# Linear attention and a gated long convolution: forward DFT ahead of the second projection, on quarters of the sequence, with all steps in a new order

## The chip, the cores and the metric

The kernel runs on one core of one Trainium2 chip. The metric is the device time of one execution in microseconds. Before the change the median of three runs is 329.52 us (328.03 to 329.56).

## What is computed

Inputs are q, k, v of shape (8 batches, 8 heads, 576 tokens, 64), a feature matrix `w_phi` (64 x 128), and for the second half `w_proj` (512 x 1536), a filter (576 x 512) and `w_out` (512 x 512). All are float32; the kernel works in bf16 with float32 sums. Per batch:

```python
def phi(x):                                   # x is q or k, per head
    p = x @ w_phi
    p = p - max(abs(p), axis=-1)
    return concat([exp(p), exp(-p)])
kv, z = phi(k).T @ v, sum(phi(k), axis=tokens)
x = (phi(q) @ kv) / (phi(q) @ z + 1e-6)        # 8 heads side by side: 576 x 512
x1, x2, x3 = split(x @ w_proj, 3)              # 576 x 512 each
conv = irfft(rfft(x2, axis=tokens) * rfft(filter, axis=tokens))
out = (x1 * conv * x3) @ w_out
```

## The kernel before, in words

The whole program is one list of words, `PLAN`. Each word is a step with its arguments: `X2,3,1@2` calls method `X2` for batch 3, chunk 1, with its result in PSUM bank 2; `#1` names one of the ring slots of a staging buffer. `run` walks through the list, and so the order of the list is the order of the instructions on every engine and on the DMA queues of SyncE (SP) and GpSimd (POOL). No scheduler changes it; the engines wait for each other through semaphores only where data or buffers require it. The words of several batches are interleaved: while batch b is in its attention part, batch b-1 is in its convolution part, and the last products of batch b-2 or b-1 are written out.

Tokens are taken as 64 groups (t) of 9 (j), so that a load of one batch is a plain block; a chunk of 128 tokens is two j of 64 t, and the ninth j makes a tail of 64 tokens. Steps of a batch, in the order of the data:

- `load`/`loadh` (L518, L524): DMA from POOL's queue, with a cast to bf16. `trh` (L534): DMA transposes on SP's queue, which turn q and k into `qT` and `kT`. For the first two batches the transposes are made on TensorE (PE) instead (`tp`, L553) and copied out of PSUM (`tpe`, L734 on ACT or L736 on DVE).
- `Pk`, `Qn` (L606, L613), `Pkt`, `Qnt` (L620): projections on `w_phi` in eight matmuls per two heads. `maxk`, `maxq` (L673): absolute maxima on VectorE (DVE). `mhi`, `mlo`, `trm` split the maxima of q in two bf16 halves and transpose them to `mT`; `Pq` (L634, L640) computes the transposed projection of q and subtracts the maxima with a selector matrix. `ex` (L657), `exkt`, `exqt`: exponentials on ScalarE (ACT). `em` (L708) writes exp of the maxima of k as a scale, and `vs` (L714) multiplies v by it on POOL.
- `KV` (L729), `KVe` (L736): sums over the tokens and their eviction. `NE`, `NEt` (L750, L759): numerator and denominator; `rc`, `xn`, `rct`, `xnt` (L764 to L781): division on DVE, giving `xn` (four chunks of 128 tokens) and `xnt` (tail). `trx`, `trxt` (L788, L793): DMA transposes on SP to `xT` and `xTt`, with the features on the partitions.
- `fold`, `foldt` (L808, L814) on POOL: the sums and differences of the two halves of the sequence, from `xT`, into `eo`. Even frequencies need only the sums, odd ones only the differences.
- `X2` (L820): second projection, 5 chunks x 4 matmuls of 512 columns, from `eo`. `X2e` (L734 on ACT, L736 on DVE): five evictions to `x2n`. `F` (L446): forward DFT from `x2n` with the tables `fwd`, `fwd5` as weights, 17 matmuls of 512 columns. `m12` (L831), `m1` (L837): products with the filter's spectrum on DVE, read straight from PSUM, into `Y` and `Y4`. `m3` (L842): the sum of the two halves of the complex product, mostly on POOL.
- `X1`, `X3` (L848), `X1t`, `X3t` (L855): first and third projection from `xT`, 16 matmuls of 512 columns each and tails; `X1e` evicts, `tm`, `tmt` (L885, L889) multiply on DVE.
- `I` (L895): inverse DFT, 24 matmuls of 288 columns; `Ie` (L898) evicts the even half on ACT, `Ip`, `Im` (L903) form sum and difference with the odd half in PSUM on DVE, into `cv`. `ym` (L914): product with x1*x3 on POOL into `yT`. `yt` puts the tails of two batches side by side. `O` (L926), `Oe` (L734), `st` (L942): last projection, eviction and stores on SP's queue.

Before the first batch, the tables are made: index rows on POOL, angles on ACT and DVE, sines on ACT (L380 to L384), masked copies on POOL (`gen_five`, L392, L394), the inverse tables as copies (`gen_inv`, L409 to L413), the forward tables as PE transposes (`tg`). The filter is loaded in 18 pieces on SP's queue, folded on POOL (`filt_fold`, L429, L431) and transformed by `H` (the same L446). `w_proj` is loaded in three parts, between other loads.

Of the kernel before, what the change touches and what calls it, by code (L numbers as in the profile page):

```python
# [16 lines left out]
SEQ = 576  # L17
# [4 lines left out]
        'rt': 2, 'xnt': 2, 'yT': 2, 'es': 2, 'cv': 2}  # L22
# [17 lines left out]
H_ev,DVE,3@7 Pqt,0@0 em,p,0,1 ex,q,m,0,1@2 Pq,0,0@4 KV,0,0@6 exqt,m,0@0 vs,p,0,1 ex,q,p,0,1@2  # L40
KVe,DVE,0,0@6 exqt,p,0@0 ex,q,m,0,0@4 vs,m,0,1 tp,q,1,1@2 Pq,0,2@0 ex,q,p,0,0@4 tpe,ACT,q,1,1@2
KV,0,1@6 ex,q,m,0,2@0 w_load,proj,1 ex,q,p,0,2@0 Pq,0,3@4 KVe,DVE,0,1@6 tp,q,1,0@3 NE,0,1@0
tpe,ACT,q,1,0@3 NE,0,0@6 rc,0,1@0 ex,q,m,0,3@4 xn,0,1@0 tp,q,1,3@2 H,1@3 rc,0,0@6 trx,0,1
ex,q,p,0,3@4 xn,0,0@6 NEt,0@0 NE,0,2@6 rct,0@0 H_ev,ACT,1@3 xnt,0,0@0 trx,0,0 NE,0,3@4 xnt,0,1@0
rc,0,2@6 H,2@0 xn,0,2@6 tpe,ACT,q,1,3@2 tp,q,1,2@1 rc,0,3@4 trx,0,2 tp,k,1,3@3 xn,0,3@4 H,4@2
tpe,ACT,k,1,3@3 tpe,DVE,q,1,2@1 H_ev,ACT,2@0 trx,0,3 Qnt,1@6 late Qn,1,0@4 maxqt,1@6 w_load,proj,2
Qn,1,2@0 maxq,1,0@4 tp,k,1,2@3 trxt,0 load,v,1 Pk,1,1@6 tpe,ACT,k,1,2@3 maxq,1,2@0 ex,k,m,1,1@6
Qn,1,1@4 ex,k,p,1,1@6 maxq,1,1@4 fold,POOL,0,1 Qn,1,3@0 X1,0,1@3 maxq,1,3@0 Pk,1,3@4 X1e,ACT,0,1@3
H_ev,ACT,4@2 fold,POOL,0,0 maxk,1,1@6 Pk,1,0@0 mhi,1 X2,0,3@3 ex,k,p,1,0@0 maxk,1,3@4 X2,0,2@2
ex,k,m,1,0@0 foldt,POOL,0,0 X2,0,0@6 foldt,POOL,0,1 X2e,ACT,0,2@2 maxk,1,0@0 load,k,3 ex,k,m,1,3@4  # L50
X2,0,4@7 mlo,POOL,1 X2e,DVE,0,3@3 load,q,2 trm,1 ex,k,p,1,3@4 X2,0,1@2 X2e,DVE,0,0@6 X2e,ACT,0,4@7
Pkt,1@0 trh,k,2,1 Pk,1,2@4 X2e,ACT,0,1@2 maxkt,1@0 X1,0,0@3 H_fix em,p,1,0 exkt,p,1@0 F,0,2@2
maxk,1,2@4 vs,p,1,0 X1e,ACT,0,0@3 F,0,0@6 em,m,1,0 exkt,m,1@0 m12,0,2@2 F,0,1@7 em,m,1,1
ex,k,m,1,2@4 F,0,4@3 vs,m,1,0 m12,0,0@6 ex,k,p,1,2@4 Pq,1,1@0 em,p,1,1 m12,0,1@7 Pqt,1@4
ex,q,m,1,1@0 F,0,3@2 vs,p,1,1 X3,0,1@6 trh,k,3,0 exqt,m,1@4 m12,0,3@2 ex,q,p,1,1@0 X3,0,0@7 tm,0,1@6
exqt,p,1@4 Pq,1,0@0 vs,m,1,1 m1,0,4@3 KV,1,0@4 ex,q,m,1,0@0 tm,0,0@7 ex,q,p,1,0@0 Pq,1,2@2
KVe,DVE,1,0@4 KV,1,1@6 m3,POOL,0,0 ex,q,m,1,2@2 Pq,1,3@4 ex,q,p,1,2@2 KVe,DVE,1,1@6 NE,1,1@0
trh,q,2,1 m3,POOL,0,1 NE,1,0@6 ex,q,m,1,3@4 rc,1,1@0 xn,1,1@0 NEt,1@2 trh,q,2,0 ex,q,p,1,3@4
rc,1,0@6 X1t,0@0 xn,1,0@6 X1te,ACT,0@0 rct,1@2 NE,1,2@6 xnt,1,0@2 trx,1,1 xnt,1,1@2 I,0,1,0@1
rc,1,2@6 NE,1,3@4 xn,1,2@6 I,0,0,0@0 trx,1,0 rc,1,3@4 X3t,0@2 xn,1,3@4 Ie,0,0@0#0 I,0,0,1@3  # L60
Ie,0,1@1#1 tmt,0@2 I,0,1,1@0 trx,1,2 Ip,0,0@3#0 I,0,2,0@1 Im,0,0@3#0 Qnt,2@6 Qn,2,0@4 Ip,0,1@0#1
Ie,0,2@1#0 Qn,2,2@2 Im,0,1@0#1 trx,1,3 X1,0,2@1 maxqt,2@6 ym,POOL,0,1 maxq,2,0@4 I,0,3,0@0
X1e,ACT,0,2@1 X1,0,3@6 trxt,1 w_load,out Ie,0,3@0#1 maxq,2,2@2 Pk,2,1@0 X1e,ACT,0,3@6 load,v,2
Qn,2,1@4 ex,k,m,2,1@0 Qn,2,3@6 maxq,2,1@4 fold,POOL,1,1 X3,0,2@2 ex,k,p,2,1@0 X1,1,1@3 maxq,2,3@6
I,0,3,1@4 X1e,ACT,1,1@3 fold,POOL,1,0 maxk,2,1@0 X3,0,3@5 mhi,2 Pk,2,3@6 Im,0,3@4#1 Pk,2,0@0
Ip,0,3@4#1 X2,1,3@3 ex,k,p,2,0@0 tm,0,2@2 foldt,POOL,1,0 foldt,POOL,1,1 X2,1,2@4 tm,0,3@5
ex,k,m,2,0@0 load,k,4 maxk,2,3@6 X2,1,0@2 X2e,ACT,1,3@3 mlo,POOL,2 ym,POOL,0,0 trm,2 X2e,ACT,1,2@4
X2,1,4@5 maxk,2,0@0 ex,k,m,2,3@6 ym,POOL,0,3 trh,k,3,1 I,0,2,1@3 X2e,DVE,1,0@2 ex,k,p,2,3@6 X2,1,1@4
load,q,3 X2e,ACT,1,4@5 Pkt,2@0 Pk,2,2@6 maxkt,2@0 X2e,ACT,1,1@4 X1,1,0@2 maxk,2,2@6 em,p,2,0
exkt,p,2@0 F,1,2@5 vs,p,2,0 X1e,ACT,1,0@2 F,1,0@4 Im,0,2@3#0 em,m,2,0 exkt,m,2@0 Ip,0,2@3#0 F,1,1@2  # L70
em,m,2,1 m12,1,2@5 ex,k,m,2,2@6 F,1,4@3 vs,m,2,0 ex,k,p,2,2@6 m12,1,0@4 Pq,2,1@0 em,p,2,1 Pqt,2@6
m12,1,1@2 ex,q,m,2,1@0 F,1,3@5 trh,k,4,0 vs,p,2,1 X3,1,1@4 exqt,m,2@6 m12,1,3@5 ex,q,p,2,1@0
X3,1,0@2 tm,1,1@4 exqt,p,2@6 Pq,2,0@0 vs,m,2,1 m1,1,4@3 KV,2,0@6 ex,q,m,2,0@0 tm,1,0@2 ex,q,p,2,0@0
Pq,2,2@4 KVe,DVE,2,0@6 KV,2,1@2 ym,POOL,0,2 ex,q,m,2,2@4 Pq,2,3@6 m3,POOL,1,0 ex,q,p,2,2@4
KVe,DVE,2,1@2 NE,2,1@0 trh,q,3,1 NE,2,0@2 ex,q,m,2,3@6 rc,2,1@0 xn,2,1@0 O,0,0@4 trh,q,3,0
ex,q,p,2,3@6 rc,2,0@2 m3,POOL,1,1 xn,2,0@2 NEt,2@0 X1t,1@5 Oe,ACT,0,0@4#0 rct,2@0 xnt,2,0@0 NE,2,2@2
trx,2,1 X1te,ACT,1@5 xnt,2,1@0 I,1,1,0@4 rc,2,2@2 NE,2,3@6 xn,2,2@2 trx,2,0 I,1,0,0@5 rc,2,3@6
X3t,1@0 xn,2,3@6 Ie,1,0@5#1 I,1,0,1@1 Ie,1,1@4#0 tmt,1@0 I,1,1,1@5 trx,2,2 Ip,1,0@1#1 I,1,2,0@4
Im,1,0@1#1 Qnt,3@2 Ip,1,1@5#0 Qn,3,0@6 Ie,1,2@4#1 Qn,3,2@0 trx,2,3 maxqt,3@2 O,0,1@4 maxq,3,0@6
X1,1,2@2 st,0,0 Im,1,1@5#0 I,1,3,0@3 maxq,3,2@0 X1e,ACT,1,2@2 ym,POOL,1,1 X1,1,3@5 trxt,2 Ie,1,3@3#0  # L80
Oe,ACT,0,1@4#1 Pk,3,1@6 X1e,ACT,1,3@5 load,v,3 Qn,3,1@2 st,0,1 Qn,3,3@0 ex,k,m,3,1@6 maxq,3,1@2
X3,1,2@4 fold,POOL,2,1 ex,k,p,3,1@6 X1,2,1@5 maxq,3,3@0 I,1,3,1@2 X1e,ACT,2,1@5 X3,1,3@3 maxk,3,1@6
fold,POOL,2,0 mhi,3 O,0,3@5 Im,1,3@2#0 Ip,1,3@2#0 Pk,3,3@0 tm,1,2@4 Oe,ACT,0,3@5#2 Pk,3,0@6
foldt,POOL,2,0 X2,2,3@2 ex,k,p,3,0@6 tm,1,3@3 foldt,POOL,2,1 load,k,5 maxk,3,3@0 X2,2,2@3
ex,k,m,3,0@6 mlo,POOL,3 ym,POOL,1,0 trm,3 X2,2,0@5 X2e,ACT,2,2@3 maxk,3,0@6 ex,k,m,3,3@0 X2,2,4@4
ym,POOL,1,3 st,0,3 X2e,DVE,2,3@2 ex,k,p,3,3@0 I,1,2,1@3 X2e,DVE,2,0@5 X2,2,1@6 load,q,4
X2e,ACT,2,4@4 O,0,2@7 X2e,ACT,2,1@6 Pkt,3@0 Oe,ACT,0,2@7#0 Pk,3,2@4 maxkt,3@0 X1,2,0@2 st,0,2
# [101 lines left out]
class Kernel:  # L189
# [258 lines left out]
    def H(self, t):  # L448
        self.dft(t, self.fe, 1)
# [550 lines left out]
```

## Time and profile before

| | |
|---|---|
| median of three runs | 329.52 us |
| the profiled execution | 332.42 us |
| its span, first to last instruction | 330.6 us |
| mean granted TensorE clock | 0.965 |
| DMA bytes moved, mean rate | 39.57 MB, 120 GB/s |

The profile comes from one execution and gives the span in several ways. *Busy time* of an engine is the time in which it had an instruction at work; PEld is the weight load of PE, which overlaps with its matmuls. A *group* line has the code line, the engine, the operation, `output<-input` with the shapes, the count, then busy time and the mean duration in ns of one instruction, then the idle time of the engine just before such instructions with what ended it. Matmuls overlap in the pipeline, so that the mean duration of one is longer than the distance from one to the next. The *chain of work* is followed back from the last instruction to whatever released each step; read forward it is a list of pieces with start, length and cause. DMA share is the mean busy share of the 16 DMA engines.

### The profile page before, as it was taken

What the parts mean: (1) busy time and instruction counts of PE and PEld (TensorE: products, weight loads), DVE (VectorE), ACT (ScalarE), POOL (GpSimd) and SP (SyncE); (2) the same over time, 40 slices, a digit from 0 to 9 for tenths busy, and PEclk for the clock granted to TensorE, in tenths of its full rate; (3) what the DMA queues carried; (4) which work ended last, traced back from release to release, by engine and by line L of the source; (5) the groups of instructions that cost most, each with busy time, mean ns of one, the idle gap of its engine ahead of it and who ended that gap; (6) DMA issues with size and microseconds to landing.
All of it is one profiled execution on the core that took longest, in us unless ns stands there. A gap on an engine that the chain in (4) does not pass through costs nothing.

```text
span 330.6 us, 9406 instructions
## 1 busy us (share of the span) xinstructions
PE 283.4 (86%) x3893; PEld 171.6 (52%) x3928; DVE 248.2 (75%) x398; ACT 226.1 (68%) x364; POOL 223.7 (68%) x186
## 2 busy tenths in 40 slices
PE   0463777898789999999997999999999989999982
PEld 0451474357434864476445754675467535844640
DVE  4487439786879698867984897988798979855750
ACT  4788766886479758984887369955896679633332
POOL 7699933794389948992979078937695749673420
PEclk9995779999999999999999899999999999999998
DMA  6778956895969887987994797996667841252146
GB/s 131 163 108 130 147 79 112 121 188 84 118 87 180 88 130 117 209 129 108 157 197 69 121 159 127 160 122 105 140 126 105 137 79 31 50 123 65 32 95 159
DMA packets 70890, 39.57 MB, mean 120 GB/s; under 512 B 51200, under 2 KB 65664, under 8 KB 70848
## 3 DMA queue, kind: packets, MB, share of 16 engines
q1 hardware_dynamic: 56032, 22.72, 38.1%
q0 software_dynamic: 14816, 16.25, 34.1%
q8 instruction: 30, 0.49, 0.6%
q14 instruction: 12, 0.10, 0.1%
HBM read 33.75 MB, written 9.44 MB: 131 GB/s over the span
## 4 chain that ended last, share of the span: by engine, by line
PE 57%; POOL 15%; DMA 11%; DVE 6%; issue 5%; ACT 4%; SPq 0%; POOLq 0%; ACTq 0%; DVEq 0%
PE ps L848 13%; PE ps L820 8%; PE ps L446 8%; PE ps L926 7%; PE ps L729 5%; PE ps L895 4%; PE ps L750 4%; DMA qT<-qn 3%; DMA xT<-xn 3%; POOL vp L714 3%; POOL vm L714 3%; DMA xTt<-xnt 2%; PE ps L634 2%; PE ps L640 2%; DMA mT<-mh 2%
## 5 line engine op out<-in xcount | busy, mean ns | idle before, releaser
L914 POOL TENSOR_TENSOR yT<-cv,x1s 128x576 bf16<-128x576 f32 x30 | 37.9, 1277 | 51.4 <-DVE cv L903 29.5
L848 PE MATMUL ps<-xT,wproj 128*128 128x512 bf16 x244 | 61.8, 380 | 2.1 <-DMA xT<-xn 1.3
L673 DVE TENSOR_REDUCE mk<-ps 128x8 f32<-128x1024 f32 (+1 forms) x40 | 43.6, 1110 | 12.4 <-PE ps L620 11.1
L673 DVE TENSOR_REDUCE mq<-ps 128x8 f32<-128x1024 f32 (+1 forms) x40 | 42.6, 1110 | 6.8 <-PE ps L613 3.5
L714 POOL TENSOR_TENSOR vp<-vn,vp 128x1152 bf16<-128x1152 bf16 x16 | 34.3, 2145 | 8.7 <-ACT vp L708 8.6
L820 PE MATMUL ps<-wproj,eo 128*128 128x512 bf16 x157 | 37.7, 380 | 2.5 <-POOL eo L814 1.5
L831 DVE TENSOR_TENSOR Y<-ps,AB 128x1024 bf16<-128x1024 f32 x32 | 36.9, 1212 | 2.9 <-PE ps L446 2.9
L657 ACT ACTIVATE Eqm<-ps 128x1024 bf16<-128x1024 f32 x32 | 33.1, 1033 | 8.0 <-PE ps L640 7.3
L808 POOL TENSOR_TENSOR eo<-xT 128x1024 bf16<-128x1024 bf16 x16 | 33.8, 2133 | 7.0 <-DMA xT<-xn 6.9
L734 ACT COPY o<-ps 128x512 f32<-128x512 f32 x36 | 21.0, 593 | 25.4 <-PE ps L926 21.7
L926 PE MATMUL ps<-wout,yT 128*128 128x512 bf16 x129 | 35.9, 385 | 2.2 <-DVE yT L914 0.9
L848 PEld LDWEIGHTS <-wproj 128*128 128x128 bf16 x256 | 23.8, 98 | 25.6
L842 POOL TENSOR_TENSOR Y<-Y 128x1024 bf16<-128x1024 bf16 x15 | 32.0, 2152 | 4.6 <-DVE Y L831 4.6
L714 POOL TENSOR_TENSOR vm<-vn,vm 128x1152 bf16<-128x1152 bf16 x16 | 34.3, 2144 | 0.0
L657 ACT ACTIVATE Ekp<-ps 128x1024 bf16<-128x1024 f32 x32 | 33.0, 1033 | 1.4 <-PE ps L606 1.3
L657 ACT ACTIVATE Ekm<-ps 128x1024 bf16<-128x1024 f32 x32 | 33.0, 1032 | 0.5 <-DVE mk L673 0.5
L657 ACT ACTIVATE Eqp<-ps 128x1024 bf16<-128x1024 f32 x32 | 33.3, 1039 | 0.0
L734 ACT CAST x1s<-ps 128x512 bf16<-128x512 f32 (+1 forms) x37 | 19.9, 538 | 18.9 <-PE ps L848 8.2
L446 PE MATMUL ps<-x2n,fwd 128*128 128x512 bf16 x134 | 31.8, 379 | 0.1
L895 PE MATMUL ps<-inv,Y 128*128 128x288 bf16 x192 | 31.1, 286 | 0.0
L898 ACT COPY es<-ps 128x288 f32<-128x288 f32 x32 | 12.0, 401 | 24.2 <-PE ps L895 13.1
L903 DVE TENSOR_TENSOR cv<-es,ps 128x288 f32<-128x288 f32 x64 | 25.6, 446 | 2.0 <-PE ps L895 1.9
(150 smaller groups left out, 593.8 us busy)
## 6 DMA issues: line engine op xcount, KB each, us to landing
out_dram<-o SPq DMA_DIRECT2D x72, 128.0 KB, 2.5
vn<-in_v_dram POOLq DMA_DIRECT2D x8, 576.0 KB, 7.8
kn<-in_k_dram POOLq DMA_DIRECT2D x7, 576.0 KB, 6.2
qn<-in_q_dram POOLq DMA_DIRECT2D x7, 576.0 KB, 8.4
wproj<-in_moe_w_proj_dram POOLq DMA_DIRECT2D x3, 512.0 KB, 6.9
fl<-in_moe_filter_fft_dram SPq DMA_DIRECT2D x18, 64.0 KB, 4.6
kn<-in_k_dram POOLq DMA_DIRECT2D x2, 288.0 KB, 6.5
qn<-in_q_dram POOLq DMA_DIRECT2D x2, 288.0 KB, 6.4
```

The lines of the kernel that those rows point to most:

```text
L446: self.mm(self.pb(0), l, r, start=(i == 0), stop=(i == len(ks) - 1))
L657: self.nc.scalar.activation(e, self.db(), AF.Exp, bias=0.0, scale=1.0 if g == "p" else -1.0)
L673: self.nc.vector.tensor_reduce(out=out, in_=src, axis=AX.X, op=ALU.max, apply_absolute_value=True)
L714: self.nc.gpsimd.tensor_tensor(out=t[:, :, :, 0:64], in0=self.at("vn", b)[:, 2 * X:2 * X + 2], in1=t[:, :, :, 64:65].to_broadcast([128, 2, ...
L734: self.nc.scalar.copy(dst, src)
L808: self.pick(eng).tensor_tensor(out=o, in0=x[:, :, :, 0, :], in1=x[:, :, :, 1, :], op=op)
L820: self.mm(self.pb(0), eo[:, kt, 128 * c:128 * c + 128], w[:, kt, 512:1024], start=(kt == 0), stop=(kt == 3))
L831: self.nc.vector.tensor_tensor(out=self.at("Y", b)[:, i, h, :], in0=self.pb(0).rearrange("p (i x) -> p i x", i=1).to_broadcast([128, 2, 512]),
L848: self.mm(self.pb(0), w[:, kt, f0 + 128 * m:f0 + 128 * m + 128], x[:, kt, :], start=(kt == 0), stop=(kt == 3))
L895: self.mm(self.pb(0, 0, 288), y, inv[:, i, :], start=(i == 0), stop=(i == 2))
L914: e.tensor_tensor(out=self.at("yT", b)[:, m, 0:SEQ], in0=self.at("cv", 4 * b + m).rearrange("p j h t -> p (j h t)"), in1=self.at("x1s", b) ...
L926: self.mm(self.pb(0), y[:, kt, 128 * j:128 * j + 128], w[:, kt, :], start=(kt == 0), stop=(kt == 3))
```

## The change

1. *The order of the two linear steps of x2 is exchanged.* A DFT over the tokens and a projection over the features commute. After the change `F` transforms `xn` itself, with the tokens on the partitions, and `X2` projects the spectrum `xf`. `F` uses the folded rows as weights and the tables as the moving operand; its result has the features on the partitions and goes through one more eviction, `Fe`, eight per batch of 288 columns; `X2` then gives 128 frequencies x 512 features in PSUM, where `m12` and `m1` read it as they read `F`'s result before. `xl` gathers the last 16 frequencies of each of the four groups into a weight for the fifth chunk of `X2`, twice side by side. `X2e` is gone.
2. *Two folds by quarters.* The token order inside a batch's chunks changes, so that a chunk's rows belong to one quarter of the sequence. `fold` forms sums (`ef`) and differences (`od`) of the halves directly from `xn`, in four instructions of 512 elements per partition; `fold2` forms sums and differences (`ee`) of the quarters from `ef`, in four of 256. An odd group of `F` is 3 matmuls of 288 columns, an even one is 2 of 144 and 1 of 288, the last of each being the unfolded tail `xnt`. The transposes of `xn` stay, for `X1` and `X3`.
3. *Layouts that follow.* `Eq`, `x1s`, `cv`, `yT`, the filter's rows and the stores have the new token order; `yt` runs for every batch into a buffer `yTt` of its own; the stores are 64 rows each as before, in pieces of 16.
4. *Tables and start.* The sines are written straight into `inv`; forward tables are PE transposes of `inv` and of small edge tables (`R`); masked copies move from POOL to DVE; the filter comes in 9 pieces. Two activations on an idle tile (`sintab`, `exptab`) are placed so that the function tables are loaded at that point, and 23 `warm` matmuls on zeros are put between the first steps.
5. *A new order of all words of `PLAN`,* which also chooses the engine anew for each movable step. Over the whole kernel, on DVE there are now 4 folds, 5 second folds, 7 `Fe`, 5 `Oe`, 3 `m3`, 1 `ym`; on POOL 28 folds, 27 second folds, 13 `m3`, 31 `ym`; on ACT 57 `Fe`, 31 `Oe`, 16 copies for `xl`. Loads of the first two batches' q and k and of the first v are in halves and earlier.

The core of the diff (the new `PLAN` is shown by its first lines and one stretch of batches 2 and 3):

```diff
+filt_load,SP,1 gen_selidx gen_rows ident gen_cols,0 zeros loadh,k,0,1 gen_cols,1 warm,2@0 sintab
+filt_load,SP,0 loadh,k,0,0 warm,4@1 loadh,q,0,1 gen_turns,0 gen_sel w_load,phi warm,4@0 gen_turns,1
+gen_angles,0 loadh,q,0,0 warm,3@1 loadh,k,1,0 warm,2@0 gen_pads gen_angles,1 gen_sin,1 loadh,q,1,0
+gen_sin,0 loadh,k,1,1 gen_ends,1 gen_sin,2 gen_selx tp,k,0,1@2 w_phi gen_ends,0 tp,k,0,0@3 warm,3@4
...
+xn,2,3@2 trh,k,4,1 I,1,1,1@4 Ie,1,1@7#0 Qn,3,0@0 fold2,POOL,2,1,0 tmt,1@5 Pk,3,0@2 Ip,1,1@4#1
+Pk,3,1@6 ex,k,p,3,0@2 fold2,POOL,2,0,0 X1,1,3@5 Im,1,1@4#1 trx,2,2 maxq,3,0@0 ym,POOL,1,1
+ex,k,m,3,0@2 O,0,0@4 trx,2,3 maxk,3,1@6 X1e,ACT,1,3@5 fold,POOL,2,0,1 I,1,0,1@1
...
-    def fold(self, eng, b, odd):
-        op = ALU.subtract if odd else ALU.add
-        x = self.at("xT", b).rearrange("p k (j h t) -> p k j h t", j=8, h=2)
-        o = self.at("eo", b)[:, :, 256 * odd:256 * odd + 256].rearrange(
-            "p k (j t) -> p k j t", j=8)
-        self.pick(eng).tensor_tensor(out=o, in0=x[:, :, :, 0, :], in1=x[:, :, :, 1, :], op=op)
...
-    def X2(self, b, c):
-        eo, w = self.at("eo", b), self.at("wproj")
+    def fold(self, eng, b, odd, p):
+        x, v = self.at("xn", b), slice(2 * p, 2 * p + 2)
+        self.pick(eng).tensor_tensor(
+            out=self.at("od" if odd else "ef", b)[:, v].rearrange("p v c x -> p v (c x)"),
+            in0=x[:, v, 0:2, :].rearrange("p v c x -> p v (c x)"),
+            in1=x[:, v, 2:4, :].rearrange("p v c x -> p v (c x)"),
+            op=ALU.subtract if odd else ALU.add)
+
+    def fold2(self, eng, b, odd, p):
+        x, v = self.at("ef", b), slice(2 * p, 2 * p + 2)
+        self.pick(eng).tensor_tensor(out=self.at("ee", b)[:, v, odd, :], in0=x[:, v, 0, :],
+                                     in1=x[:, v, 1, :], op=ALU.subtract if odd else ALU.add)
...
+    def X2(self, b, t):
+        xf, w = self.at("xf", b), self.at("wproj")
         for kt in range(4):
-            self.mm(self.pb(0), eo[:, kt, 128 * c:128 * c + 128], w[:, kt, 512:1024],
-                    start=(kt == 0), stop=(kt == 3))
-
-    def X2e(self, eng, b, c):
-        self.copy(eng, self.at("x2n", b)[:, c, :], self.pb(0))
-
-    def F(self, b, t):
-        self.dft(t, self.at("x2n", b), 0)
+            l = xf[:, kt, t, 0:128] if t < 4 else self.at("xl", b)[:, kt, :]
+            self.mm(self.pb(0), l, w[:, kt, 512:1024], start=(kt == 0), stop=(kt == 3))
+
+    def F(self, b, v, odd):
+        t = self.at("xnt", b)[:, 2 * (v // 2):2 * (v // 2) + 2, :].rearrange("p u d -> p (u d)")
+        acc = self.pb(0, 0, 288)
+        if odd:
+            o = self.at("od", b)[:, v]
+            for k in range(2):
+                self.mm(acc, o[:, k, :], self.tab(2 * k, 1), start=(k == 0), stop=False)
+        else:
+            e = self.at("ee", b)[:, v]
+            for k in range(2):
+                part = lambda x: x.rearrange("p (s f) -> p s f", s=2)[:, :, 72 * k:72 * k + 72]
+                self.mm(part(acc), e[:, k, :], part(self.tab(0, 0)), start=(k == 0), stop=False)
+        self.mm(acc, t, self.tab(1 + 2 * (v % 2), odd), start=False, stop=True)
+
+    def Fe(self, eng, b, v, odd):
+        self.copy(eng, self.at("xf", b)[:, v, 2 * odd:2 * odd + 2, :].rearrange(
+            "p g x -> p (g x)"), self.pb(0, 0, 288))
...
+    def sintab(self):
+        z = self.at("idle")[0:1, 0:1]
+        self.nc.scalar.activation(self.at("junk"), z, AF.Sin, bias=0.0, scale=1.0)
```

## The prediction

> **What bounds the kernel now.** I read the page's busy shares first, then the busy time by stage, then the chain of work, then the groups, then each engine's timeline of the first 60 us. Shares alone:
>
> ```profile
> PE 283.4 (86%) x3893; PEld 171.6 (52%) x3928; DVE 248.2 (75%) x398; ACT 226.1 (68%) x364; POOL 223.7 (68%) x186
> PE 57%; POOL 15%; DMA 11%; DVE 6%; issue 5%; ACT 4%; SPq 0%; POOLq 0%; ACTq 0%; DVEq 0%
> ```
>
> PE leads both the shares and the chain, but 86% is a mean over unlike stages. By stage (length, then busy us of PE, PEld, DVE, ACT, POOL, granted clock, DMA share, GB/s):
>
> ```profile
> 0.00:60.00 60.00, 33.29 (x512) 23.73 (x517) 37.34 (x72) 43.20 (x66) 43.82 (x59) 0.86 0.75 127
> 60.00:100.00 40.00, 34.16 (x485) 19.53 (x487) 30.84 (x46) 27.99 (x44) 26.66 (x23) 1.00 0.79 116
> 100.00:320.00 220.00, 211.93 (x2882) 126.65 (x2907) 179.74 (x281) 152.02 (x251) 153.24 (x106) 0.99 0.71 117
> 320.00:330.60 10.60, 4.02 (x17) 1.67 (x18) 0.28 (x2) 2.93 (x5) 0.00 (x0) 0.87 0.69 161
> ```
>
> Two kernels in one. In the first 60 us PE is idle for 26.7 us and POOL and ACT are busiest. From 100 to 320 PE is busy 211.9 of 220 us: there a microsecond of PE work is nearly a microsecond of time. From the start of one batch's forward DFT to the next:
>
> ```profile
> 100.00:134.20 34.20, 33.25 (x475) 20.01 (x479) 29.18 (x45) 25.89 (x44) 26.44 (x21) 1.00 0.92 133
> 134.20:168.50 34.30, 33.10 (x476) 19.92 (x479) 29.05 (x46) 25.59 (x42) 25.09 (x19) 1.00 0.96 153
> ```
>
> PE 33.1, DVE 29.1, ACT 25.7, POOL 25.8 of 34.3 us. DVE is next, 4 us behind.
>
> **Steady state, PE.** The durations of matmuls overlap (the groups' means are latencies), so I price by start-to-start, from the chain in order of time (start, length, what):
>
> ```profile
> 78.50 0.47 PE ps L759 x8
> ...
> 302.59 3.68 PE ps L446 x17
> ...
> 310.57 1.10 PE ps L895 x9
> ```
>
> One whole forward DFT of a batch is the second line: 17 matmuls of 512 columns in 3.68 us, 0.216 each. A 288-column matmul is 1.10/9 = 0.122. Of 130 columns: 0.47/8 = 0.059. No 144-column one is in the trace; it lies between 0.059 and 0.122, and by the line between them it is 0.065. The new forward DFT has per batch 4 chunks x (odd: 3 of 288; even: 2 of 144 and 1 of 288): 16 x 0.122 + 8 x 0.065 = 2.47 us. Gain 3.68 - 2.47 = 1.21 us a batch, **9.7 us** in eight. By the bounds of the 144-column price it is 8.1 to 10.1. Nothing else on PE changes in number: X2 keeps 20 x 512 columns, O its 144, the inverse its 192; Pq, NE and O only read or write in another order. The 56 additional weight loads (24 for 17 a batch) lie beside matmuls, as PEld does now. 23 `warm` matmuls (23 x 0.216 = 5.0 us) stand in the first stages, where PE has 26.7 us of idle time; if that cover were gone they would cost those 5 us.
>
> **Steady state, the others.** These rows price it:
>
> ```profile
> L898 ACT COPY es<-ps 128x288 f32<-128x288 f32 x32 | 12.0, 401 | 24.2 <-PE ps L895 13.1
> L734 ACT CAST x2n<-ps 128x512 bf16<-128x512 f32 x24 | 14.0, 600 | 6.2 <-PE ps L820 6.0
> L736 DVE CAST x2n<-ps 128x512 bf16<-128x512 f32 x16 | 10.4, 683 | 2.0 <-PE ps L820 2.0
> L808 POOL TENSOR_TENSOR eo<-xT 128x1024 bf16<-128x1024 bf16 x16 | 33.8, 2133 | 7.0 <-DMA xT<-xn 6.9
> L814 POOL TENSOR_TENSOR eo<-xTt 128x128 bf16<-128x128 bf16 x15 | 6.1, 425 | 10.0 <-DMA xTt<-xnt 10.0
> ```
>
> ACT: 57 evictions of 288 at 0.401 (22.9) and 16 `xl` copies of 256 elements (priced by the 373 ns of the 128x256 x1s cast: 6.0) for 24 of 512 (14.4) and 5 Oe (3.0): +11.5 us, 1.4 a batch, to 27. DVE: 16 evictions of 0.683 go (10.9); 7 Fe at about 0.45, 5 Oe, 2 m3 (0.68 each), 4 folds, 5 second folds (under 0.5 each by m3's 0.68 for 1024) and 4 `yt` come: about +12; level, 29. POOL: by the two rows above, 0.181 + 0.00191 per element; 512 elements 1.16, 256 elements 0.67. 28 folds (32.4) and 27 second folds (18.1) for 16 + 15 (40.2): +10; less 2 m3 (4.3), less table building (below): 1 a batch more, to 27. All three stay under a PE period of 34.3 - 1.2 = 33.1, but closer. I let PE's idle time in a period (34.3 - 33.1 = 1.2) grow by 0.4: **+3 us** over seven periods; bounds 0 and 8.5 (the whole gain of seven periods given back).
>
> The wait that goes is the fold's on the transposes of xn (POOL eo<-DMA xT 6.9, xTt 10.0 us of idle). Today a batch goes xn, DMA transpose (4 to 8 us on the chain), fold, X2, DFT; after it goes xn, fold, DFT, Fe, X2. The transposes remain for X1 and X3 alone, which have slack. What is late next: POOL works in order, and a fold now queues behind `ym`, which today waits 29.5 us in all on DVE's cv and 19.0 on PE. F waits for the fold, Fe and X2 for F. Price under the rivals.
>
> **The Trainium skill on DVE beside POOL.** Where DVE reads two SBUF inputs it may slow POOL: of the two `Y<-Y` sums on POOL at 213.3 us, in 4.72 us together instead of 4.2, the first began while DVE's yT product (two SBUF inputs, 1.39 us) still ran; at 318.2 POOL's yT kept its 1.28 us beside the same product. "GPSIMD Engine Reference", Key points, states that POOL shares its SBUF interfaces with VectorE and contends with such instructions; one place here agrees and one does not. It speaks against the 12 folds and m3 now on DVE, some 5 us in all; by the rule the sum would be at most 5 us of POOL longer, by the second place nothing.
>
> **Start.** POOL carries it: one unbroken run from 11.5 to 43.4 us. Its first `vp` product starts at 34.9, the last ends at 43.3; the first xn follows at 47.4, the folds at 56.6, X2 at 58.8. The change takes from POOL the eight masked tables (L392/394, 5.0 us), three copies to `inv` (1.5), and the two tail folds of the filter (2.5 for one copy, 0.6). In the new order POOL has ahead of its first `vp`: index tables and identity 3.4, 13 load issues at 0.79 (10.3), selector 1.5 + 2.1, memsets 0.9, filter folds 4.9 + 0.6, `inv` 2.0 = 25.7 us. ACT must deliver the scale exp(max) by then: one table load fewer, sines straight into `inv`; its list up to there is some 20 us of rows, starting at 3.3 with a wait of a few us for the q halves, so 24 to 25. The first `vp` moves from 34.9 to 26, and what follows it is bound by ACT's and DVE's lists of the first batch (eight Eq at 0.92, the maxima at 1.05, start-to-start), which I follow to the first batch's last xn at 42 instead of 52. F then needs no transpose, but waits for POOL's eight folds (7.3 us). I take **-8.5 us**. Bounds: 0 (the loads, which for the first 60 us move the same bytes, set the pace: DMA share 0.75 there; w_proj comes a third after a third as before) and -14 (folds and F fully under way at 45).
>
> PE's granted clock is 0.70, 0.61 and 0.83 in the three tens from 20 to 50 us, where PE is busy 18.8 us; some 5 us of that is clock. "TensorE: Matmul & The Clock Gate", Part 1, states a default of half rate, lifted after about 3.4 us of sustained work; by it the early `warm` matmuls help. The trace grants 1.00 from 0 to 20 with PE idle until 12, so I take nothing for them.
>
> **Tail.** The last X3 to the end is 14 us now (chunk product on PE to 316.7, tm, cv, yT to 320.1, five O, evictions, stores to 330.6) and keeps its form; a second POOL product in place of DVE's costs 0.6, two evictions on DVE save as much. **0**.
>
> **Sum.** The profiled execution took 332.4 us (span 330.6 and 1.8 around it): 332.4 - 9.7 - 8.5 + 3 = 317.2. The median of the three runs, 329.52, is 0.9913 of the profiled one; so **314**.
>
> **Rivals.** (a) *Only one gain.* If DVE (29 of 34, with many short waits) or the new order sets the period, the PE time saved becomes PE idle: 332.4 - 8.5 = 323.9, that is 321. If the loads hold the start, 332.4 - 9.7 + 3 = 325.7, that is 323. For: DVE is 4 us behind PE; DMA share 0.92 to 0.96 in two periods. Against: PE was served at 97% from such a margin. Case at 322. (b) *Slower: the fold chain on POOL.* Eight folds are 7.3 us in order on POOL behind four `ym` that wait for cv; the transposes that they replace took 4 to 8 us, with nothing of an engine. If 4 us of it stand open in each of seven periods, 28 us come against 18.2 saved and (9.7 + 8.5): 332.4 - 18.2 + 28 = 342.2, that is 339. It decides from 18.2/7 = 2.6 us a period. For: POOL idles 51.4 us ahead of yT now, longest 7.5, so a thing behind it is held. Against: F stands among the next batch's Pk, Qn and this batch's I and O, which can fill PE. (c) *Given back, no change*: 1.3 to 2.6 us a period open, about 329. (d) *More than forecast*: the start gains 14 and no new wait: 332.4 - 9.7 - 14 = 308.7, that is 306, and lower with a better order in the 6 us of PE idle from 60 to 100.
>
> **Numbers.** Forecast 0.50 (314, own range 307 to 320); (a) 0.22; (b) 0.13; (c) 0.07; (d) 0.08. One sign holds most. Half a per cent, 1.6 us, is about what a measurement of this kernel can tell from no change. Faster: 0.50 + 0.08 + 0.20 = 0.78; same: 0.07 and a little of (a) = 0.09; slower: 0.13. The range takes in (a), (c) and the bounds of (d): 302 to 331; above lies (b), below some 0.03.
>
> **What would show it.** F groups on PE: some 2.5 us per batch at 0.122 a step; first `vp` on POOL near 26, last xn of the first batch near 42; the distance from one batch's DFT to the next near 33.5; PE over 94% busy from 90 us on. Wrong: PE idle before F on POOL's folds (rival b), DVE over 93% (a), q or w_proj loads ahead of PE before 50 us (a), PE clock below 0.9 after 60 us.

## The result

The changed kernel takes 376.5 us (median of 4, 372.3 to 377.75) against 329.54 us of the kernel before on the same chip: ratio 1.141, 95% interval 1.131 to 1.151. It is **slower by 47 us**, where 314 was forecast in a range of 302 to 331. Ratios here and below are formed from undisturbed executions only, so that one can differ a little from the quotient of two medians.

The page of the changed kernel, shares and chain:

```profile
PE 297.3 (79%) x3968; PEld 181.9 (48%) x4010; DVE 259.5 (69%) x432; ACT 228.4 (61%) x402; POOL 226.4 (60%) x199
PE 52%; DMA 25%; DVE 9%; SPq 5%; ACT 4%; issue 3%; DVEq 0%; POOL 0%; ACTq 0%
```

Every engine's share fell, and DMA on the chain went from 11% to 25%. The engines' busy times grew by 2 to 14 us (PE most, from 283.4 to 297.3, at a lower granted clock), the span by 45: most of the loss is waiting, and the part of it that grew is for transfers. POOL, which the rival with the exposed folds needs on the chain, went from 15% to 0. By stage (the same first three stretches as before; length, then busy us of PE, PEld, DVE, ACT, POOL, granted clock, DMA share, GB/s):

```profile
0.00:60.00 60.00, 34.45 (x489) 22.95 (x493) 37.59 (x93) 35.71 (x56) 39.19 (x50) 0.80 0.75 127
60.00:100.00 40.00, 35.12 (x521) 21.79 (x525) 36.14 (x53) 32.17 (x57) 30.55 (x28) 0.98 1.05 138
100.00:320.00 220.00, 188.04 (x2684) 115.54 (x2713) 157.93 (x236) 145.63 (x255) 141.13 (x109) 0.91 0.65 101
320.00:375.40 55.40, 39.68 (x281) 21.65 (x282) 27.81 (x52) 14.87 (x36) 15.53 (x14) 0.90 0.30 78
```

The steady state, where PE was busy for 211.9 of 220 us before, is now busy for 188.0, at a clock of 0.91 instead of 0.99. The waits say on what (engine, tile and line, released by: us in all, times, longest):

```profile
POOL mh L746 <- ACT mh L741: 37.1, 5, 15.5
ACT o L781 <- DMA out_dram<-o: 25.6, 6, 12.2
...
DVE mq L720 <- PE ps L663: 18.1, 5, 14.4
DVE wphi L507 <- DMA phi<-in_w_phi_dram: 16.0, 1, 16.0
DVE o L783 <- DMA out_dram<-o: 15.7, 4, 7.9
```

Two kinds of line are new in this size. `o <- out_dram` is an output eviction that waits until an earlier store has read its buffer out: 25.6 us on ACT and 15.7 on DVE, against 2.0 in all in the kernel before:

```profile
ACT o L734 <- DMA out_dram<-o: 2.0, 2, 1.2
```

`wphi <- phi` is the first copy of w_phi, which waits 16 us. The other two pass a wait on, since each engine takes its instructions in the order of the list. The longest of each show it: ACT's eviction to `o` waits 12.2 us and starts at 141.7 us; behind it PE, then DVE's `mq` (14.4 us, until 146.0) and POOL's `mh` (15.5 us, until 148.0) stand idle. The long pieces of the chain in order of time (start, length, what) show the same places, and add transposes:

```profile
8.89 15.92 DMA phi<-in_w_phi_dram
...
90.13 8.64 DMA xT<-xn
...
130.00 11.63 DMA out_dram<-o
...
181.04 13.71 DMA mT<-mh
...
351.06 8.62 DMA out_dram<-o
...
361.10 7.13 DMA out_dram<-o
```

In the kernel before, a store landed in a median of 2.5 us after its issue (the last number):

```profile
out_dram<-o SPq DMA_DIRECT2D x72, 128.0 KB, 2.5
```

Here single ones hold the chain for 7 to 12 us, though they carry the same 128 KB; the page gives no median for them. The last 27 us show how they run. Forty slices of 348.0 to 375.4 us, DMA share in tenths and GB/s:

```profile
DMA  0222222222232222222222222222222258832000
GB/s 15 42 69 99 84 63 27 54 75 81 99 69 78 93 99 102 102 102 102 90 57 84 99 102 75 81 102 102 99 90 102 105 126 170 278 120 84 33 0 0
```

and the tail of the kernel before, 318.0 to 330.6 us:

```profile
DMA  0000698879892069797979798989797979600000
GB/s 0 0 0 0 169 215 208 189 195 208 202 215 65 0 156 202 195 221 182 215 189 215 189 208 202 215 202 208 202 215 176 228 182 228 137 0 0 0 0 0
```

Stores alone are in flight in both. Before, the 16 DMA engines are 60 to 90% busy, at about 200 GB/s; after, 20%, steadily, at about 100 GB/s. That looks like a transfer that uses some of the engines only.

**Theory S.** The new stores write their 64 rows as 4 runs of 16 (`"(q t j) f -> q j t f"[c, i:8:2]`), and the filter's new loads read theirs in the same way. By this theory a pattern whose outermost count is 4 runs on 4 of 16 engines. **Rival O**: the new order of all steps, with POOL's folds in the path of `F`, makes the loss, and the stores are late only because of it.

### The profile page after: what moved, and what is told of

Same layout as the page of the kernel before. It is cut to its first block, busy times and chain, and to the rows that moved or that the text cites. A ratio compares the mean times of both kernels' runs of the same rounds, so it can differ in the third digit from the quotient of the medians.

```text
span 375.4 us, 9600 instructions
## 1 busy us (share of the span) xinstructions
PE 297.3 (79%) x3968; PEld 181.9 (48%) x4010; DVE 259.5 (69%) x432; ACT 228.4 (61%) x402; POOL 226.4 (60%) x199
## 4 chain that ended last, share of the span: by engine, by line
PE 52%; DMA 25%; DVE 9%; SPq 5%; ACT 4%; issue 3%; DVEq 0%; POOL 0%; ACTq 0%
DMA out_dram<-o 13%; PE ps L914 11%; PE ps L875 9%; PE ps L776 5%; PE ps L1000 5%; DMA phi<-in_w_phi_dram 4%; PE ps L967 4%; PE ps L795 4%; DMA mT<-mh 4%; DMA xT<-xn 2%; PE ps L921 2%; PE ps L656 2%; PE ps L649 2%; PE ps L683 2%; PE ps L677 2%
## 5 line engine op out<-in xcount | busy, mean ns | idle before, releaser
L914 PE MATMUL ps<-xT,wproj 128*128 128x512 bf16 x238 | 65.6, 392 | 4.4 <-DMA xT<-xn 2.5
L720 DVE TENSOR_REDUCE mq<-ps 128x8 f32<-128x1024 f32 (+1 forms) x40 | 44.2, 1112 | 23.2 <-PE ps L663 18.1
L761 POOL TENSOR_TENSOR vp<-vn,vp 128x1152 bf16<-128x1152 bf16 x16 | 34.3, 2147 | 14.4 <-ACT vp L755 14.4
L781 ACT COPY o<-ps 128x512 f32<-128x512 f32 x31 | 18.3, 598 | 37.2 <-DMA out_dram<-o 25.6
L897 DVE TENSOR_TENSOR Y<-ps,AB 128x1024 bf16<-128x1024 f32 x32 | 38.4, 1216 | 3.4 <-PE ps L875 3.3
L1000 PE MATMUL ps<-wout,yT 128*128 128x512 bf16 x117 | 33.6, 400 | 3.0 <-POOL yT L984 2.3
L973 DVE TENSOR_TENSOR cv<-es,ps 128x288 f32<-128x288 f32 x64 | 27.1, 446 | 8.4 <-PE ps L967 6.9
L850 POOL TENSOR_TENSOR od<-xn 128x512 bf16<-128x512 bf16 x16 | 18.6, 1165 | 23.2 <-DVE xn L814 14.5
L875 PE MATMUL ps<-wproj,xf 128*128 128x512 bf16 x123 | 31.8, 383 | 0.4
L908 POOL TENSOR_TENSOR Y<-Y 128x1024 bf16<-128x1024 bf16 x13 | 28.3, 2182 | 5.3 <-DVE Y L897 5.2
L967 PEld LDWEIGHTS <-Y 128*128 128x128 bf16 x192 | 17.7, 98 | 22.1 <-issue 12.7
```

The source lines that it names most:

```text
L720: self.nc.vector.tensor_reduce(out=out, in_=src, axis=AX.X, op=ALU.max, apply_absolute_value=True)
L761: self.nc.gpsimd.tensor_tensor(out=t[:, :, :, 0:64], in0=self.at("vn", b)[:, 2 * X:2 * X + 2], in1=t[:, :, :, 64:65].to_broadcast([128, 2, ...
L781: self.nc.scalar.copy(dst, src)
L875: self.mm(self.pb(0), l, w[:, kt, 512:1024], start=(kt == 0), stop=(kt == 3))
L897: self.nc.vector.tensor_tensor(out=self.at("Y", b)[:, i, h, :], in0=self.pb(0).rearrange("p (i x) -> p i x", i=1).to_broadcast([128, 2, 512]),
L908: self.pick(eng).tensor_tensor(out=Y[:, 0:2, :], in0=Y[:, 0:2, :], in1=Y[:, 2:4, :], op=ALU.add)
```

## The experiments

### One-level rows, in the new kernel and in the old

**Stores and filter.** Four kernels on one chip. The first two write, or write and read, 64 rows in one level; the third only moves two loads; the last puts the new pattern into the kernel before. The code cuts in this and the next sections are shortened.

```diff
 storerow and bothrow
-rows = self.out[b].rearrange("(q t j) f -> q j t f", q=4, j=9)[c, i:8:2]
+rows = self.out[b].rearrange("(t j) f -> j t f", j=9)[2 * c + i]
 bothrow
-rows = self.dram["filt"].rearrange("(q t j) d -> q j t d", q=4, j=9)     # [2 * h + i, a:8:2]
+rows = self.dram["filt"].rearrange("(t j) d -> j t d", j=9)              # [2 * (2 * h + i) + a]
 phifirst: PLAN
-filt_load,SP,1 gen_selidx ... gen_sel w_load,phi warm,4@0
+w_load,phi filt_load,SP,1 gen_selidx ... gen_sel warm,4@0
 before_store4
-self.nc.sync.dma_start(out=rows[4 * (c % 2) + 2 * i + c // 2], in_=o[64 * i:64 * i + 64, :])
+self.nc.sync.dma_start(out=self.out[b].rearrange("(q t j) f -> q j t f", q=4, j=9)[c, i:8:2],
+                       in_=o[64 * i:64 * i + 64, :])
```

> The changed kernel with one edit: each store writes its 64 rows through a one-level row pattern of 64 (as the kernel before does) in place of 4 runs of 16 rows; same bytes, same number of stores, the same place in the order. The rows land at other tokens' places. Theory S (the stores in 4 runs use a quarter of the DMA engines, hold the o buffers, and Oe on ACT and DVE waits in order for them): landing falls from 5 to 12 us to about 2.5, the waits of o on out_dram (25.6 + 15.7 us) go, the tail of 28 us falls to about 15; the start stays late (first vp near 40, phi landed near 25): 376 - 45 = about 331, bounds 325 to 342. Theory O (the new order of the steps, with POOL's fold chain, makes the loss by itself): 365 or more.

Measured 342.05 us, ratio 1.041 (1.036 to 1.047). That is 10 hundredths of the 14 lost, about 33 us, from one line that changes neither bytes nor counts nor order. The stores land in 2.4 us:

```profile
out_dram<-o SPq DMA_DIRECT2D x72, 128.0 KB, 2.4
```

Rival O (365 or more) is out as the main cause. But 342 is the far end of what theory S gave, and 9.3 + 5.4 us of waits for `out_dram` are left.

> As the run with one-level stores, and the eight 64-row filter loads too read 64 rows in one level in place of 4 runs of 16, so the filter's rows stand in another order. Theory S: the filter lands sooner, w_phi behind it on the same queue by about 14 us in place of 24.9, first vp near 30, start 8 to 12 us sooner: about 320, bounds 314 to 328, which is faster than the kernel before. Theory O: 365 or more; if only the stores are to blame and the late start comes from the new order, the same time as the run with one-level stores alone (about 331).

Measured 336.54 us, ratio 1.023 (1.018 to 1.028). The copy of w_phi waits 4.2 us instead of 16.0, the first product with v on POOL starts at 31.9 us instead of 40.2. That is about 6 us, not 8 to 12, and above the given bounds of 314 to 328.

> The changed kernel with w_phi's two loads issued on SP ahead of the filter's nine instead of behind them; nothing else moves. Theory S: DVE's wait of 16.0 us at the copy of phi goes, the first vp comes 8 to 14 us sooner, the stores stay slow: 376 - 11 = about 365, bounds 360 to 371. Rival: the filter itself comes too late then (its first cast is on POOL, ahead of gen work there), and the start is not shorter: 374 to 380.

Measured 366.31 us, ratio 1.113 (1.106 to 1.121): 9 us, as theory S expected. w_phi is 32 KB, but it is queued on SP behind eight loads that crowd on few engines.

> The kernel before with one edit: its stores write their 64 rows as 4 runs of 16 rows, as the changed kernel does; the same bytes and number, rows land at other tokens' places. Theory S: landing goes from 2.5 us to 5 to 12, the o buffers are held and the tail grows by about 10 us: 329.5 + 20 to 50, near 360. Theory O (the pattern costs nothing, the order does): 329 to 332.

Measured 356.6 us, ratio 1.082 (1.073 to 1.090). The kernel before has neither the folds by quarters nor the new order, and loses 27 us by the pattern alone. Here the loss shows less as waits for `o` than as transposes queued behind stores (7% of its chain is the transpose of the tail, `xTt<-xnt`). Its tail runs like that of the changed kernel, 344.0 to 356.4 us:

```profile
DMA  2223597897422222232222222222222211000000
```

### How many engines

Is it the outermost count, the length of the pieces, or the mere second level? The kernel before with 8 runs of 8 rows and with 2 of 32:

```diff
+self.nc.sync.dma_start(out=self.out[b].rearrange("(t z j) f -> j z t f", z=8, j=9)[2 * c + i],   # z=2
+                       in_=o[64 * i:64 * i + 64, :])
```

> The kernel before with its stores writing 64 rows as 8 runs of 8 rows (rows at other tokens' places). Theory S (the outermost count sets the number of engines): half the rate of 64 rows in one level, landing about 3.5 us, time 331 to 338. If it is the pieces' size or the mere second level that costs: as with 4 runs of 16, 350 or more.

> The kernel before with its stores writing 64 rows as 2 runs of 32 rows (rows at other tokens' places). Theory S: half the engines of 4 runs of 16, so clearly more than its 356.6: 390 to 450, and some 50 GB/s in the tail where 4 runs moved 90 to 100. If larger pieces are better: less than 356.

Measured 345.19 us (ratio 1.049, 1.039 to 1.058) and 413.13 us (1.255, 1.243 to 1.267). Long pieces are the worst. 8 runs cost more than expected, by 7 us above the given bound; still, the order 64, 8, 4, 2 holds throughout. The last 29.6 us with 2 runs, share and rate:

```profile
DMA  1111111111115741111111111111111111111000
GB/s 55 50 50 50 53 53 50 50 53 53 50 50 152 186 127 50 50 53 53 50 50 53 53 50 50 50 50 55 50 50 50 53 53 50 50 53 47 22 0 0
```

and the last 12.6 us with 8 runs:

```profile
DMA  5445554453245555547988524455435445100000
GB/s 111 104 189 202 195 195 163 182 182 124 85 143 182 156 195 195 189 182 228 254 267 228 176 85 85 137 202 176 163 117 163 150 176 182 72 0 0 0 0 0
```

The share is 0.1, 0.2 and 0.4 to 0.5 for 2, 4 and 8 runs, near 2/16, 4/16 and 8/16, and the rate about 50, 100 and 180 GB/s: 23 to 25 GB/s for each engine used. (The short peaks are the tails' stores, which have 64 rows in one level in these kernels too.) With 64 rows in one level it is 200 GB/s at shares of 0.6 to 0.9; there SP's issue, 0.56 to 0.6 us for 128 KB, is nearly the limit (128 KB by 0.58 us is 226 GB/s).

The single packets in the traces show the number itself. In the last 13, 6 and 3 us of stores with 2, 4 and 8 runs, the packets of 2 KB in flight at once are 2 for 85% of the time, 4 for 72%, and 7 to 9 for 75% (8 for 44%). With 64 rows in one level up to 16 are in flight. With 2, 4 and 8 runs a packet takes 0.084 us in the median, which is 24 GB/s.

The Trainium skill states this rule: "DMA: Bandwidth & Descriptors", section "Why a DMA increments its semaphore by 16 and not by 1", says that a transfer uses the largest number of engines up to 16 that divides the size of the slowest dimension (of those larger than one) of both access patterns, and on SP's and ACT's queues always the lowest-numbered ones. The runs agree with the number; in all of them the SBUF side has 64 rows outermost, so that only the DRAM side was varied. That the same few engines are taken each time was not read from a trace, but it would explain why other transfers queue behind such stores.

### Every row at its place

The runs with one-level rows put rows elsewhere. To keep each row at its place, the 16 groups have to be outermost in DRAM, and the rows of `o` must come in the same order. So the product ahead of it writes its columns in that order:

```diff
-self.pick(eng).tensor_tensor(out=self.at("yT", b)[:, m, :, :], in0=cv, in1=x1s, op=ALU.mult)
+for h in range(2):
+    self.pick(eng).tensor_tensor(out=y[:, m, h, 0:256].rearrange("p (q t k) -> p q k t", q=4, k=4),
+                                 in0=n(c[:, h, 0:256]), in1=n(x[:, m, h, 0:256]), op=ALU.mult)
+self.nc.vector.tensor_tensor(out=yTt[:, m, a:a + 64], in0=c[:, :, 256:288], in1=x[:, m, :, 256:288], ...)
 st
-rows = self.out[b].rearrange("(q t j) f -> q j t f", q=4, j=9)[c, i:8:2]
+rows = self.out[b].rearrange("(q t j) f -> q t j f", q=4, j=9)[c, :, i:8:2]
```

> The changed kernel with every output row at its place: POOL's product writes yT with the 16 token groups outermost (two instructions of 256 columns instead of one of 576, the tails by a small product on DVE into yTt in place of the copy), so that each store of 64 rows writes DRAM as 16 x 4 x 512 instead of 4 x 16 x 512; w_phi first; the filter's loads stay in 4 runs. Theory S (the outermost count decides how many engines a transfer uses): stores land in about 2.5 us as with one-level rows, 342 - 10 = about 332, bounds 326 to 340. If only one level of rows is fast, not 16 x 4: 360 or more.

Measured 337.15 us, ratio 1.025 (1.022 to 1.029), against 366.31 us and 1.113 of the run that has w_phi first alone. The store still has two levels of rows, 16 x 4 instead of 4 x 16, and lands in 2.4 us:

```profile
out_dram<-o SPq DMA_DIRECT2D x72, 128.0 KB, 2.4
```

Here too up to 16 packets are in flight at once. So it is not the second level of rows that costs; the outermost count fits all five patterns.

### What else kept the forecast away

With stores, filter and w_phi mended, 314 is still far. Three runs on one chip:

> The run with one-level stores and one-level filter loads (rows at other tokens' places, the filter's rows in another order), and besides w_phi's loads ahead of the filter's on SP. Theory S: the two repairs of the start overlap, w_phi was still waited for 4.2 us: about 333, bounds 329 to 337. If the whole late start was w_phi: 326 to 329. The forecast of 314 needs more than the layouts.

> As the run before in this list, with 4 buffers for o instead of 3 (and 3 for r instead of 4, to make room). If what is left above the forecast is that Oe waits in order for an o buffer that a store behind three transposes still holds (13 us of waits on out_dram, one of 7.8 us with PE idle and its clock at 0.53 after it): 8 to 12 us less than without, about 323. If it is the rest of the new order: within 3 us of it.

> As the first run in this list, without the 23 warming matmuls on the zero tile (they add nothing to the result). If they lie in idle time of PE, as the prediction has it: within 1.5 us. If they cost PE time: 3 to 5 us less. If they keep the clock up in the first 60 us: 2 to 5 us more.

Ratios 1.0115 (1.005 to 1.018), 0.991 (0.985 to 0.997) and 1.0001 (0.996 to 1.004); medians 333.45, 330.15 and 328.88. The first is as expected. One place of it is left in the chain:

```profile
110.16 4.67 SPq L833 DMA_TRANSPOSE xT<-xn  x3
114.93 1.26 SPq L1012 DMA_DIRECT2D out_dram<-o  x2
```

```profile
115.03 0.53 SPq L1012
115.56 0.05 issue
115.61 8.33 DMA out_dram<-o
...
124.04 0.59 ACT o L781
124.64 0.04 issue
124.68 0.88 PE ps L967 x3
```

```profile
110.00:125.00 15.00, 5.82 (x58) 3.49 (x56) 6.10 (x10) 5.73 (x13) 7.06 (x8) 0.85 1.24 175
```

First fence: SP's queue, where the store is issued behind transposes of `xn`. Second: the chain, where the store then takes 8.33 us. Third: that stretch, with a DMA share over 1 (q, k and v loads beside them) and PE busy 5.8 of 15 us. The store has 64 rows in one level here and is late all the same; that this comes from the transposes ahead of it and from full DMA queues is read from their order and was not tested by itself. Three `o` buffers don't cover it. With a fourth the ratio is 2 hundredths lower; but the ten times of that run spread from 323.68 to 333.46 us, and it also changed `r`. So it was repeated with `r` as it was, on top of the run without warming matmuls:

> The run without warming matmuls (one-level stores and filter loads, so rows at other tokens' places; w_phi first), with 4 buffers for o in rotation and all 4 of r. (In the earlier run with 4 buffers of o and 3 of r, a reciprocal was overwritten before its use in places, so that its output was another and some of its waits may have been.) If Oe's wait for an o buffer held by a store behind three transposes is what is left: 328.9 - 6 = about 323, bounds 320 to 325. If not: 327 to 330.

Ratio 0.983 (0.975 to 0.991), 322.75 us: 1.7 hundredths (5.5 us) below the run without warming matmuls alone. The wait for `o` was the next limit: ACT's and DVE's waits for it, 5.7 and 4.2 us without the fourth buffer, are 0 and 2.2 us with it.

Between the runs with and without the 23 warming matmuls lie 1.1 hundredths, 3.7 us, and the two intervals only just stand apart (329.62 to 334.36 us in 4 runs, 325.68 to 333.2 in 10). The traces put none of this where those matmuls stand. The first `X2`, which comes after the last of them, starts at the same time, with them (first line) and without; what differs is a wait for an `o` buffer later on (third line with, fourth without):

```profile
56.74 1.89 PE L875 MATMUL ps<-wproj,xf 128*128 128x512 bf16 x8
56.82 1.89 PE L874 MATMUL ps<-wproj,xf 128*128 128x512 bf16 x8
ACT o L781 <- DMA out_dram<-o: 9.7, 2, 9.0
ACT o L780 <- DMA out_dram<-o: 5.7, 2, 5.0
```

From there to the first `X2` of batch 7 it takes 242.8 us with and 239.3 without. So a cost of the warming matmuls themselves is not shown; how they could change a wait 50 us later is open.

### All in one

```diff
 RING: 'o': 3 -> 'o': 4, slots of Oe dealt out in turn; no warm words; w_load,phi first; yT as above,
-self.nc.vector.tensor_tensor(out=yTt ...)
+self.pick(eng).tensor_tensor(out=yTt ...)                       # on POOL with the rest of ym
```

> The changed kernel with every output row at its place, and four edits: stores of 16 x 4 rows through the reordered yT (the tails' small product now on POOL instead of DVE, where 64 elements took 0.739 us beside POOL's product), w_phi first, no warming matmuls, 4 buffers for o in rotation instead of 3. Theory S with the o buffers as the next limit: 337.2 for the version with stores and w_phi mended, less 3 to 4 (warming matmuls), less 6 to 7 (o buffers), less 0 to 3 (DVE): about 325, bounds 321 to 330. If the o buffers gained nothing and what is left is the order: 332 or more.

**321.83 us, ratio 0.977 (0.971 to 0.983)**: every row at its place, and faster than the kernel before and the changed one. Its steady state beside that of the kernel before, 100 to 300 us, this kernel first:

```profile
100.00:300.00 200.00, 196.92 (x2779) 120.22 (x2778) 165.61 (x256) 147.50 (x266) 152.34 (x165) 0.99 0.68 119
```

```profile
100.00:300.00 200.00, 192.73 (x2757) 116.64 (x2782) 165.40 (x258) 145.41 (x238) 146.06 (x101) 0.99 0.76 124
```

PE is fuller than before, and a batch takes less time. From the first `X2` matmul of batch 0 to that of batch 7 it takes 288.9 - 60.7 = 228.2 us, against 296.0 - 58.8 = 237.2 before and 334.6 - 68.8 = 265.8 in the changed kernel as it was given. What is still missing to the forecast of 314 was looked for in the start. Two more runs:

> The version with all four edits, and the filter's eight 64-row loads in one level of rows (the filter's rows in another order). Its first second projection starts at 60.7 us, held by a k load of 15.0 us that shares DMA engines with the filter's pieces. Theory S: k lands in 6 to 8 us, the first second projection near 56.5, 4 us less in all: about 318, bounds 315 to 320. If the start is held by the amount of loads and not by how the filter's are spread: 320 to 323.

> The version with all four edits, and each 64-row load of the filter as four of 16 rows, so that every row stays at its place and each load has 16 rows outermost; SP issues 33 loads instead of 9 (24 x 0.56 = 13 us more of SP). Theory S: as with one-level rows if SP's issues are in time (the second half of the filter is needed near 23 us): about 318 to 320. If SP's issues come too late: 321 to 326.

Ratios 0.964 (0.956 to 0.971; 318.06 us) and 0.980 (0.973 to 0.986; 323.11 us). With the filter on all engines the first `X2` comes at 56.0 instead of 60.7 us, and 4 us are won. In 33 loads of 16 rows, each row in its place, it comes at 59.9 and nothing is won: SP is busy issuing them until 22.2 us, against 8.4 us with 9 loads, which would use up the gain. A layout of the filter that has both was not tried.

## Why the prediction was wrong

1. **The step that failed** is one that the sum did not have. The prediction named what the change does to arithmetic, evictions, tables and order, and took the new stores as unchanged: they are in no term, its tail stands at **0**, and of the loads of the start it says that they "move the same bytes". Bytes, count and order were the same; the outermost count went from 64 to 4. Stores that land in a median of 2.5 us hold the chain for 5 to 12. In place of nothing the runs showed about 33 us for the stores (1.141 to 1.041) and some 10 us for filter and w_phi together (1.041 to 1.0115): 43 of the 47 us lost. The sign is not explained by them alone: with both mended the kernel is still at 1.0115, and falls clearly below 1 only with a fourth `o` buffer (0.983). That three buffers do not cover a late store is the second thing the sum did not have.
2. *F on PE, -9.7 us*: right where it runs densely. In the run with one-level rows and w_phi first, two `L883` take 0.24 us, one `L889` 0.12, two `L888` 0.13, as priced (0.122 and 0.065):

```profile
110.89 0.24 PE ps L883 x2
111.13 0.12 PE ps L889
...
128.92 0.13 PE ps L888 x2
129.05 0.12 PE ps L889
```

   The estimate for 144 columns, by a line between 130 and 288, held. Its lower bound was reckoned wrongly: with 0.122 for 144 columns the gain is 6.0 us, not 8.1. The 9.7 us as a whole were not measured apart from the rest.
3. *Start, -8.5*: POOL's list was read rightly and the start was not. With w_phi first and one-level filter loads the first product with v starts at 27.3 us (forecast 26, 40.2 in the changed kernel), but the divisions to `xn` end at 48.0, not at 42, and `X2` begins at 56.7 instead of 58.8: a gain of 2. The bound of 0, "the loads set the pace", was there; it was the nearer one. The DMA share is 0.92 to 1.02 from 10 to 40 us there, and the clock 0.57 between 30 and 40. How the missing 6 us divide between loads and ACT's and DVE's lists stays open.
4. *Closer engines, +3*: right only with an edit that the change does not have. The way from the first `X2` of batch 0 to that of batch 7 was to shrink by 8.5 - 3 = 5.5 us. With stores, filter and w_phi mended it grows by 5.6 (299.5 - 56.7 = 242.8, against 237.2 before), with a long wait for `o` in it. In the run with a fourth `o` and no warming matmuls it shrinks by 5.6 (288.2 - 56.6 = 231.6), in the version with all edits by 9.0. These are single profiled executions.
5. *Tail, 0*: from the end of the last inverse product (351.4) to the end of the span it is 24 us; before it was 13 (317.8 to 330.6). Two stores of 8.62 and 7.13 us stand in the chain there, each ahead of an eviction that waits for its buffer. In the version with all edits it is 25.3 us from the last matmuls of `X2` (295.4) to the end, in the kernel before 30.8, in the changed kernel 33.4 (342.0): the form of the tail was not the cost.
6. *Warming matmuls, nothing*: the traces of the start agree (first `X2` at 56.74 us with them, 56.82 without). The 3.7 us between the two runs arise later, and their cause is open. The reason given was wrong, though: the clock of 1.00 that the prediction read from 0 to 20 us is not PE's speed there. In the kernel before, 18 transposes of 128 columns from 15.57 us on take 1.97 us, about 0.1 each, against 0.059 for 130 columns later. In the changed kernel the warming matmuls of 512 columns start about 0.42 us apart until 6.2 us and 0.21 apart after it: half the speed for the first 4 us.
7. *Rivals*: (b) named "slower" with the fold chain on POOL as its mechanism. The sign came, the mechanism did not: none of the long waits of the changed kernel is PE for a fold, and POOL is at 0% of its chain. (a) was half there, in the start. That the stores could get slower was in no rival, though the change lists them "in pieces of 16".

## What to carry to other kernels

Read a DMA's access pattern as an engine count: the outermost size larger than one decides over how many of the 16 engines it spreads (2, 4, 8, 16 and 64 rows on the DRAM side were run here), and a change of layout that keeps every byte can cut it to a quarter. When the order of rows has to change, let an instruction ahead of the store arrange the data so that a multiple of 16 stands outermost, as the 16 x 4 rows did here. The sign in a profile is a DMA share that stays flat at a simple fraction (0.1, 0.2, 0.5) while transfers are waited for; and a slow store is paid where its buffer is wanted next, by an in-order engine and all that stands behind it.

## What the runs showed that was not expected

- *DVE and POOL in each other's way, which the prediction's sum took as nothing.* The four selector instructions on POOL take 3.70 us at 5.0 us in the changed kernel, where DVE rounds the angles at the same time (conversion 0.93 us, a product with two SBUF inputs 1.36 us), and 1.06 us in the kernel before at another time. A copy of the tails on DVE took 0.198 us before and 0.896 in the mean after: four of the eight still 0.22 or 0.23, one 4.09, with POOL's products around it:

```profile
L783 DVE COPY yTt<-yT 128x256 bf16<-128x256 bf16 x8 | 7.2, 896 | 1.5 <-POOL yT L984 1.4
```

   In the version with the reordered `yT` the product of 64 elements took 0.739 us on DVE beside POOL's product; on POOL, in its turn, 0.306:

```profile
L991 DVE TENSOR_TENSOR yTt<-cv,x1s 128x64 bf16<-128x64 f32 x32 | 23.7, 739 | 0.2
```

   The Trainium skill, "GPSIMD Engine Reference", section "Key points", says that the two share SBUF interfaces, with contention when DVE has two SBUF inputs or uses a two-port mode. The selector instructions beside DVE's product and the 64-element product, which have two SBUF inputs on DVE, agree, as far as two engines at work at the same time show it; the copy has one input, and no run shows its mode. None of it was tested by itself.
- *A wait costs its length and then clock.* In the run with one-level rows and w_phi first, PE waits for 9.2 us until 124.7 us; its granted clock is 0.65 from 124.6 to 128.5 us and 1.00 from there to 135 us, with PE busy nearly throughout; the changed kernel's mean over the whole span is 0.899, against 0.965 before and 0.971 in the version with all edits.
